# A later q, sums on GpSimd and a grouped weight decode in the prologue of an attention and expert kernel

## The chip, the cores and the metric

One core of a Trainium2 chip runs the whole kernel. The metric is the device time of one execution in microseconds. Three runs of the kernel before gave 1012.68, 1017.62 and 1015.35 us, median 1015.35.

## What is computed

For 8 batches of 8 heads, 576 tokens and 64 head dimensions, attention goes through 32 memory slots; its output is the input of two expert layers.

```
a    = softmax(phi, over the 576 tokens)
k_m  = a^T k;  v_m = a^T v                      # 32 slots per head
attn = softmax(q k_m^T / 8, over the 32 slots)
x    = attn v_m                                 # 4608 tokens x 512
y    = max(x w1, x w2, x w3) w_out              # 512 -> 768 -> 512
out  = the expert of the largest gate: relu(y e_w1) e_w2, times its gate
```

The weights w1, w2, w3, w_out and the experts' are float64 in memory.

## The kernel before, in words

Every product with float32 data is made of three float32r products of a high and a low part: `mm3` (L99) issues them, `split` (L95) makes the parts, the high one as a copy on ScalarE, the low one as a subtraction on VectorE (on GpSimd for h of batches 1 to 7).

The kernel has two stages: attention with the first expert layer, batch by batch (L889), then the second layer (L981). A batch's attention output stays in its factored form: `at_out` gives the attention weights in `at_hi`, `at_lo`; `u_step` (L407) multiplies one sixth (index f) of w1, w2, w3 with v_m into `u`; `m1_step` (L435) multiplies both for one f, one half of the tokens (hf) and one of the three matrices (i). Matrix 0's result is copied to `hx` by ScalarE (L448), those of 1 and 2 go into `hx` as a running maximum on VectorE (L450); then hx is split. `m2_step` or, for half of batch 0, `m2_by_f` multiplies with w_out. The results of all these products share four PSUM banks.

Weights come as 24 parts of 512 KB: parts 3f, 3f+1, 3f+2 are w1, w2, w3 of index f, parts 18 to 23 are w_out. Each is loaded by the SP queue into one of six raw buffers (L180, `bufs=NRAW`), and decoded from 64-bit words in five instructions: an absolute value on ScalarE (L150), then on VectorE two steps with one input (L153, L160) and two with two inputs (L163, L166). w_out's parts are also split. `w_done(n)` writes the decode of part n and, from part 2 on, the load of part n+6. Parts 0 to 5 are decoded ahead of the batches, while the attention of batch 0 runs; parts 6 to 23 in batch 0's m1 steps, three per f (L916), 6 and 7 only after batch 0's scores (`scored`). `after(t, src)` is a one-element copy on ScalarE into a tile: what overwrites the tile must wait for it, and it waits for src.

The attention of batch b+1 is written between the products of batch b. A `Stream` (L758) holds pairs of a due time and a function; each product step advances its time (0.97 per m1 step), and what is due is written there. The due times are in AT (L56) and, for batch 1, AT1 (L58). In batch 0's stream the loads of phi, k, v and q of batch 1 are added with their own due times and conditions (L895 to L897): phi after part 10 is decoded, k and v after part 13, q after part 15. `load_next_q(b)` (L393) loads q of batch b+1 at the due time of batch b's last q transpose (L370): batch 2's q is loaded with batch 1's attention, that is, during batch 0's products. `prefetch` (L399) does so for phi, k and v.

`at_asum` (L252) sums the exponentials over nine chunks by `over_chunks` (L214): four two-input instructions over 512, 256, 128 and 128 columns, on VectorE; the same helper gives the maxima. `at_qT` (L310) transposes one of four q tiles on VectorE.

The order in which each engine gets its instructions is not the written one: a planner goes by its own estimate of when inputs and engine are ready, and by the written order among those that are. The order is fixed when the program is built; on the chip every engine works down its list.

Of the kernel before, what the change touches and what calls it, by code (L numbers as in the profile page):

```python
# [8 lines left out]
F32 = mybir.dt.float32  # L9
# [10 lines left out]
def kernel(  # L20
# [37 lines left out]
    AT1 = dict(max=18, col=19, sub=20.5, q=(30, 31, 32, 33), exp=22, asum=23, km=31, kvT=33, sc=36,  # L58
               smax=(38, 39.5), sexp=(39.5, 41), ssum=(42, 44), out=(45, 47))
    XN = 256  # L60
# [111 lines left out]
    wraw, wdst = {}, {}  # L172

    def w_load(n, src=None):
        if n >= len(wparts):
            return
        part = wparts[n]
        if isinstance(part, tuple):
            f, i = part
            t = sp.tile([P, J, P], U64, tag="w64", name="w64", bufs=NRAW)  # L180
            if src is not None:
                after(t.bitcast(F32)[:, 0, 0:1], src)
            nc.sync.dma_start(
                out=t, in_=(w1, w2, w3)[i][:, f * P:(f + 1) * P].rearrange("(j p) f -> p j f", p=P)
            )
            t = t.rearrange("p j f -> p (j f)")
        else:
            t = sp.tile([P, DM], U64, tag="w64", name="w64", bufs=NRAW)
            nc.sync.dma_start(out=t, in_=w_out[part * P:(part + 1) * P, :])
        wraw[n] = t  # L190

    def w_dst(n):
        part = wparts[n]
        if n in wdst:
            return
        if isinstance(part, tuple):
            wdst[n] = w123[:, part[0], part[1]].rearrange("p j f -> p (j f)")
        else:
            wdst[n] = sp.tile([P, DM], F32, tag="wod", name="wod", bufs=2)

    def w_a(n):
        w_dst(n)
        decode_a(wdst[n], wraw[n])

    def w_b(n):
        part = wparts[n]
        decode_b(wdst[n], wraw[n])
        if not isinstance(part, tuple):
            split(wo_hi[:, part], wo_lo[:, part], wdst[n])
# [4 lines left out]
    def over_chunks(dst, t, op):  # L214

        h = ep.tile([P, J, 4, M], F32, tag="hc", name="hc")
        nc.vector.tensor_tensor(out=h, in0=t[:, :, 0:4], in1=t[:, :, 4:8], op=op)
        nc.vector.tensor_tensor(out=h[:, :, 0:2], in0=h[:, :, 0:2], in1=h[:, :, 2:4], op=op)
        nc.vector.tensor_tensor(out=dst, in0=h[:, :, 0], in1=t[:, :, 8], op=op)
        nc.vector.tensor_tensor(out=dst, in0=dst, in1=h[:, :, 1], op=op)  # L220

    def at_max(b):
        t = inp["phi", b]
        mx = ep.tile([P, J, M], F32, tag="mx", name="mx")
        over_chunks(mx, t, ALU.max)
        st["mx", b] = mx
# [25 lines left out]
    def at_asum(b):  # L252
        t = inp["phi", b]
        asum = ep.tile([P, J, M], F32, tag="mx", name="asum")
        over_chunks(asum, t, ALU.add)
        st["asum", b] = asum
# [53 lines left out]
    def at_qT(b, j):  # L310

        if ("qT", b) not in st:
            st["qT", b] = ep.tile([P, J, NCH, 2, 32], F32, tag="qT", name="qT")
        nc.vector.transpose(
            out=st["qT", b][:, j].rearrange("p c e d -> p (c e d)"), in_=inp["q", b, j].rearrange("p c d -> p (c d)")
        )
# [49 lines left out]
    def attention(b):  # L366

        T = AT if b > 1 else AT1
# [7 lines left out]
            (T["q"][J - 1], lambda: load_next_q(b)),  # L376
# [16 lines left out]
    def load_next_q(b):  # L393
        if b + 1 < B:
            for j in range(J):
                load_q(b + 1, j)
# [421 lines left out]
    with ExitStack():  # L818
        def w_done(n, src=None):
            if src is not None:  # L820
                w_dst(n)
                after(wdst[n][:, 0:1], src)
            w_a(n)
            w_b(n)
            if n >= 2 and n + NRAW < len(wparts):
                w_load(n + NRAW)
# [57 lines left out]
        def start_step():  # L884
            if started[0] < len(wparts):
                w_done(started[0], scored if started[0] < 8 else None)
                started[0] += 1

        for b in range(B):  # L889
            stream = Stream(attention(b + 1) if b + 1 < B else [])  # L890
            if b > 0:
                stream.add([(2, lambda: gate_a(b - 1)), (5, lambda: gate_b(b - 1)), (11.5, lambda: gate_c(b - 1))])
            else:
                done = lambda n: wdst[n][0:1, 0:1]
                stream.add([(10, lambda: load_phi(1, done(10)))])  # L895
                stream.add([(16 + i, lambda i=i: load_kv(1, i, done(13))) for i in range(2)])
                stream.add([(20 + j, lambda j=j: load_q(1, j, done(15))) for j in range(J)])  # L897
            for f in range(NF1):
# [13 lines left out]
                for hf in range(2):  # L912
                    for i in range(3):
                        m1_step(b, f, hf, i)
                        if b == 0 and (hf, i) in ((0, 0), (0, 2), (1, 1)):
                            start_step()  # L916
                        if b == 0 and 0 < f < NF1 - 1 and (hf, i) == (1, 0):
                            u_step(0, f + 1)
                        stream.advance(0.97)
            if b == 0:  # L920
                while started[0] < len(wparts):
                    start_step()
# [135 lines left out]
```

## Time and profile before

| | |
|---|---|
| time of three runs, median | 1015.35 us |
| time of the profiled execution | 1014.16 us |
| its span, first to last instruction | 1012.4 us |
| TensorE busy | 978.7 us (97%) |
| VectorE busy | 562.1 us (56%) |
| ScalarE busy | 370.5 us (37%) |
| GpSimd busy | 149.9 us (15%) |

The span is the time from the first to the last instruction of one execution. Busy shares are over the whole span; matmuls are pipelined and their ends are modelled, so the gaps between them are partly hidden in their busy time. In the rows below PE is TensorE, DVE VectorE, ACT ScalarE, POOL GpSimd, SPq the SP queue; L163 is line 163 of the kernel before, and a value in brackets is the time for which the engine had been idle before an instruction, with what ended it.

### The profile page before, as it was taken

To read this page: it belongs to the slowest core of one execution; us is meant where nothing else is said; L and a number is where in the kernel's file an instruction comes from. 1 tells how busy PE (TensorE), PEld (TensorE's weight loads), DVE (VectorE), ACT (ScalarE), POOL (GpSimd) and SP (SyncE) were. 2 spreads that over 40 slices of the span, in tenths; PEclk is the share of its full clock that TensorE was granted. 3 is DMA by queue.
4 is the path that set the end of the run, shared out by engine and by line. 5 is a ranking of instruction groups with operands and counts; after the bars stand their busy time and mean duration, and the time that the engine had idled before them with its cause. 6 is when DMAs were issued, how large, how long until landed. Compare 5 with 4: busy or idle time off the path is not lost. (4 is left out here: it accounts for less than half of the span.)

```text
span 1012.4 us, 20551 instructions
## 1 busy us (share of the span) xinstructions
PE 978.7 (97%) x8306; PEld 854.6 (84%) x8306; DVE 562.1 (56%) x1289; ACT 370.5 (37%) x808; POOL 149.9 (15%) x259
## 2 busy tenths in 40 slices
PE   7888999999999999999999999999999999999996
PEld 4466788879888898988989989898989898989885
DVE  6889877473674737657165727171717171716341
ACT  2555343333433324334245415050506060604130
POOL 0000012110211102112021130202021212121110
PEclk9899999999999999999999999999999999999999
DMA  8487423132221322110117417171717161615030
GB/s 288 135 259 262 141 66 103 47 130 83 75 92 48 131 83 75 46 47 2 48 61 251 164 40 221 35 226 32 229 32 228 33 212 49 211 45 151 22 110 22
DMA packets 59107, 114.79 MB, mean 113 GB/s; under 512 B 7687, under 2 KB 20999, under 8 KB 59008
## 3 DMA queue, kind: packets, MB, share of 16 engines
q1 hardware_dynamic: 48480, 94.01, 28.5%
q0 software_dynamic: 4768, 9.94, 4.2%
q10 hardware_dynamic: 5760, 9.48, 2.5%
q8 instruction: 67, 1.10, 0.5%
q14 instruction: 32, 0.26, 0.1%
HBM read 94.00 MB, written 19.44 MB: 112 GB/s over the span
## 5 line engine op out<-in xcount | busy, mean ns | idle before, releaser
L100 PE MATMUL ps_m<-at_hi,u_hi 128*128 128x288 f32 x576 | 177.9, 310 | 6.9 <-ACT hx L448 3.2
L102 PE MATMUL ps_m<-at_hi,u_lo 128*128 128x288 f32 x576 | 170.5, 297 | 0.2 <-ACT u_lo L427 0.2
L101 PE MATMUL ps_m<-at_lo,u_hi 128*128 128x288 f32 x576 | 170.3, 296 | 0.1
L100 PE MATMUL ps_x<-yh,w1h 128*128 128x288 f32 (+1 forms) x544 | 160.3, 295 | 0.2 <-DVE xh L617 0.2
L101 PE MATMUL ps_x<-yl,w1h 128*128 128x288 f32 (+1 forms) x544 | 159.9, 294 | 0.0
L102 PE MATMUL ps_x<-yh,w1l 128*128 128x288 f32 (+1 forms) x544 | 159.8, 294 | 0.0
L97 POOL TENSOR_TENSOR h_lo<-hx,h_hi 128x288 fp32r<-128x288 f32 x84 | 72.9, 868 | 466.3 <-ACT h_hi L96 462.3
L100 PEld LDWEIGHTS ps_m<-at_hi,u_hi 128*128 128x128 f32 x576 | 108.2, 189 | 37.3 <-issue 14.2
L646 POOL DMA_DIRECT2D out_dram<-o x144 | 71.1, 500 | 346.2 <-DVE o L643 306.0
L450 DVE TENSOR_TENSOR hx<-hx,ps_m 128x288 f32<-128x288 f32 x192 | 85.5, 448 | 65.2 <-PE ps_m L102 40.9
L100 PE MATMUL ps_m<-h_hi,wo_hi 128*128 128x288 f32 x384 | 115.1, 300 | 1.9 <-DVE hx L450 1.8
L101 PE MATMUL ps_m<-h_lo,wo_hi 128*128 128x288 f32 x384 | 113.2, 295 | 0.0
L102 PE MATMUL ps_m<-h_hi,wo_lo 128*128 128x288 f32 x384 | 113.0, 295 | 0.0
L102 PEld LDWEIGHTS ps_m<-at_hi,u_lo 128*128 128x128 f32 x576 | 108.7, 189 | 1.4 <-ACT u_lo L427 0.7
L101 PEld LDWEIGHTS ps_m<-at_lo,u_hi 128*128 128x128 f32 x576 | 108.7, 189 | 1.2 <-issue 1.0
L643 DVE TENSOR_SCALAR o<-ps_x,scal 128x512 f32<-128x512 f32 x32 | 24.0, 751 | 151.6 <-PE ps_x L102 151.6
L100 PE MATMUL ps_x<-w2h,xh 128*128 128x512 f32 x272 | 107.7, 396 | 0.0
L101 PE MATMUL ps_x<-w2l,xh 128*128 128x512 f32 x272 | 107.5, 395 | 0.0
L102 PE MATMUL ps_x<-w2h,xh 128*128 128x512 f32 x272 | 107.4, 395 | 0.0
L100 PEld LDWEIGHTS ps_x<-yh,w1h 128*128 128x128 f32 x544 | 102.3, 188 | 1.5 <-DVE xh L617 0.5
L101 PEld LDWEIGHTS ps_x<-yl,w1h 128*128 128x128 f32 x544 | 102.1, 188 | 0.6 <-ACT yl L732 0.2
L102 PEld LDWEIGHTS ps_x<-yh,w1l 128*128 128x128 f32 x544 | 102.1, 188 | 0.0
(200 smaller groups left out, 1593.6 us busy)
## 6 DMA issues: line engine op xcount, KB each, us to landing
raw<-in_moe_w_dram SPq DMA_DIRECT2D x72, 512.0 KB, 4.7
raw<-y_dram SPq DMA_DIRECT2D x36, 288.0 KB, 3.1
w<-in_moe_w_dram SPq DMA_DIRECT2D x18, 512.0 KB, 5.1
kv_t<-in_k_dram SPq DMA_DIRECT2D x8, 1152.0 KB, 7.1
kv_t<-in_v_dram SPq DMA_DIRECT2D x8, 1152.0 KB, 9.8
q_t<-in_q_dram SPq DMA_DIRECT2D x32, 288.0 KB, 3.0
y_dram<-y_sb ACTq DMA_DIRECT2D x32, 288.0 KB, 2.1
out_dram<-o POOLq DMA_DIRECT2D x144, 64.0 KB, 1.9
```

Source lines behind the costliest of these rows:

```text
L97: eng.tensor_tensor(out=dst_lo, in0=src, in1=dst_hi, op=ALU.subtract)
L100: nc.tensor.matmul(out=ps, lhsT=hi_l, rhs=hi_r, start=first, stop=False)
L101: nc.tensor.matmul(out=ps, lhsT=hi_l, rhs=lo_r, start=False, stop=False)
L102: nc.tensor.matmul(out=ps, lhsT=lo_l, rhs=hi_r, start=False, stop=last)
L450: nc.vector.tensor_tensor(out=hx[0], in0=hx[0], in1=ps, op=ALU.max)
L643: nc.vector.tensor_scalar(out=o, in0=ps, scalar1=scal[:, b, t:t + 1], scalar2=None, op0=ALU.mult)
L646: nc.gpsimd.dma_start(out=out5[b, half, c], in_=o[i:i + TB])
```

## The change

- Parts 6 to 17, the three matrices of one f, are decoded by one call: four groups, each of one ScalarE and four VectorE instructions over 1536 columns in place of 512. The six raw buffers become one tile with six slots, so that three lie side by side. A group is written at the first m1 step of f = 0 to 3; parts 18 and 19 then follow in f = 3, 20 to 22 in f = 4 and 23 in f = 5. The loads of the three parts that reuse a group's slots are written after the group.
- The sum of exponentials of batch 1 runs on GpSimd.
- q of batch 2 is loaded after batch 1's attention output (at_hi) is there, with a condition on it, in place of with batch 1's q transposes; its four transposes are due at 12.7 to 15.7 in batch 1's stream in place of 0 to 5, and wait for h_hi of batch 1, f = 1. As `load_next_q` goes by the same due times, q of batch 3 is loaded later, too.
- In batch 1's schedule the maximum is due at 17 in place of 18; its phi waits for part 9 in place of 10, k and v for part 12 in place of 13.

```diff
--- before.py
+++ after.py
@@ -55,8 +55,9 @@
 
     AT = dict(max=1, col=4.5, sub=6.5, q=(0, 2, 3.5, 5), exp=9, asum=11, km=16.5, kvT=18, sc=20.5,
               smax=(24.5, 27), sexp=(29, 31), ssum=(34, 37), out=(41.5, 45))
-    AT1 = dict(max=18, col=19, sub=20.5, q=(30, 31, 32, 33), exp=22, asum=23, km=31, kvT=33, sc=36,
+    AT1 = dict(max=17, col=19, sub=20.5, q=(30, 31, 32, 33), exp=22, asum=23, km=31, kvT=33, sc=36,
                smax=(38, 39.5), sexp=(39.5, 41), ssum=(42, 44), out=(45, 47))
+    AT2 = dict(AT, q=(12.7, 13.7, 14.7, 15.7))
     XN = 256
     TT0 = [t * P for t in range(NTT - 1)] + [S - P]
     QK = 1.0 / float(D) ** 0.5
@@ -169,60 +170,59 @@
 
 
     wparts = [(f, i) for f in range(NF1) for i in range(3)] + list(range(NF1))
-    wraw, wdst = {}, {}
+    wdst = {}
+    raw64 = sp.tile([P, NRAW, DM], U64, name="raw64")
 
     def w_load(n, src=None):
         if n >= len(wparts):
             return
         part = wparts[n]
+        t = raw64[:, n % NRAW]
         if isinstance(part, tuple):
             f, i = part
-            t = sp.tile([P, J, P], U64, tag="w64", name="w64", bufs=NRAW)
             if src is not None:
-                after(t.bitcast(F32)[:, 0, 0:1], src)
+                after(t.bitcast(F32)[:, 0:1], src)
             nc.sync.dma_start(
-                out=t, in_=(w1, w2, w3)[i][:, f * P:(f + 1) * P].rearrange("(j p) f -> p j f", p=P)
+                out=t.rearrange("p (j f) -> p j f", j=J),
+                in_=(w1, w2, w3)[i][:, f * P:(f + 1) * P].rearrange("(j p) f -> p j f", p=P),
             )
-            t = t.rearrange("p j f -> p (j f)")
         else:
-            t = sp.tile([P, DM], U64, tag="w64", name="w64", bufs=NRAW)
             nc.sync.dma_start(out=t, in_=w_out[part * P:(part + 1) * P, :])
-        wraw[n] = t
-
-    def w_dst(n):
+
+    def w_dst(n, m):
         part = wparts[n]
         if n in wdst:
             return
         if isinstance(part, tuple):
-            wdst[n] = w123[:, part[0], part[1]].rearrange("p j f -> p (j f)")
+            wdst[n] = w123[:, part[0], part[1]:part[1] + m].rearrange("p i j f -> p (i j f)")
         else:
             wdst[n] = sp.tile([P, DM], F32, tag="wod", name="wod", bufs=2)
 
-    def w_a(n):
-        w_dst(n)
-        decode_a(wdst[n], wraw[n])
-
-    def w_b(n):
+    def w_a(n, m):
+        w_dst(n, m)
+        decode_a(wdst[n], raw64[:, n % NRAW:n % NRAW + m].rearrange("p a f -> p (a f)"))
+
+    def w_b(n, m):
         part = wparts[n]
-        decode_b(wdst[n], wraw[n])
+        decode_b(wdst[n], raw64[:, n % NRAW:n % NRAW + m].rearrange("p a f -> p (a f)"))
         if not isinstance(part, tuple):
             split(wo_hi[:, part], wo_lo[:, part], wdst[n])
 
 
     st = {}
 
-    def over_chunks(dst, t, op):
+    def over_chunks(dst, t, op, eng):
 
         h = ep.tile([P, J, 4, M], F32, tag="hc", name="hc")
-        nc.vector.tensor_tensor(out=h, in0=t[:, :, 0:4], in1=t[:, :, 4:8], op=op)
-        nc.vector.tensor_tensor(out=h[:, :, 0:2], in0=h[:, :, 0:2], in1=h[:, :, 2:4], op=op)
-        nc.vector.tensor_tensor(out=dst, in0=h[:, :, 0], in1=t[:, :, 8], op=op)
-        nc.vector.tensor_tensor(out=dst, in0=dst, in1=h[:, :, 1], op=op)
+        eng.tensor_tensor(out=h, in0=t[:, :, 0:4], in1=t[:, :, 4:8], op=op)
+        eng.tensor_tensor(out=h[:, :, 0:2], in0=h[:, :, 0:2], in1=h[:, :, 2:4], op=op)
+        eng.tensor_tensor(out=dst, in0=h[:, :, 0], in1=t[:, :, 8], op=op)
+        eng.tensor_tensor(out=dst, in0=dst, in1=h[:, :, 1], op=op)
 
     def at_max(b):
         t = inp["phi", b]
         mx = ep.tile([P, J, M], F32, tag="mx", name="mx")
-        over_chunks(mx, t, ALU.max)
+        over_chunks(mx, t, ALU.max, nc.vector)
         st["mx", b] = mx
 
     def at_col(b):
@@ -252,7 +252,7 @@
     def at_asum(b):
         t = inp["phi", b]
         asum = ep.tile([P, J, M], F32, tag="mx", name="asum")
-        over_chunks(asum, t, ALU.add)
+        over_chunks(asum, t, ALU.add, nc.gpsimd if b == 1 else nc.vector)
         st["asum", b] = asum
 
     def at_km(b):
@@ -311,6 +311,9 @@
 
         if ("qT", b) not in st:
             st["qT", b] = ep.tile([P, J, NCH, 2, 32], F32, tag="qT", name="qT")
+        if b == 2:
+
+            after(st["qT", b][:, j, 0, 0, 0:1], hs[1, 1][0].bitcast(F32)[0:1, 0:1])
         nc.vector.transpose(
             out=st["qT", b][:, j].rearrange("p c e d -> p (c e d)"), in_=inp["q", b, j].rearrange("p c d -> p (c d)")
         )
@@ -365,7 +368,7 @@
 
     def attention(b):
 
-        T = AT if b > 1 else AT1
+        T = {1: AT1, 2: AT2}.get(b, AT)
         L = [
             (T["max"], lambda: at_max(b)),
             (T["col"], lambda: at_col(b)),
@@ -373,7 +376,7 @@
         ]
         L += [(T["q"][j], lambda j=j: at_qT(b, j)) for j in range(J)]
         L += [
-            (T["q"][J - 1], lambda: load_next_q(b)),
+            (T["q"][J - 1] if b > 1 else T["out"][1] + 0.2, lambda: load_next_q(b)),
             (T["exp"], lambda: (at_exp(b, 0), at_exp(b, 1))),
             (T["asum"], lambda: at_asum(b)),
             (T["km"], lambda: at_km(b)),
@@ -393,7 +396,7 @@
     def load_next_q(b):
         if b + 1 < B:
             for j in range(J):
-                load_q(b + 1, j)
+                load_q(b + 1, j, st["at_hi", 1].bitcast(F32)[0:1, 1, 0:1] if b == 1 else None)
 
     def prefetch(b):
         if b < B:
@@ -816,14 +819,15 @@
             return t
 
     with ExitStack():
-        def w_done(n, src=None):
+        def w_done(n, src=None, m=1):
             if src is not None:
-                w_dst(n)
+                w_dst(n, m)
                 after(wdst[n][:, 0:1], src)
-            w_a(n)
-            w_b(n)
-            if n >= 2 and n + NRAW < len(wparts):
-                w_load(n + NRAW)
+            w_a(n, m)
+            w_b(n, m)
+            for i in range(n, n + m):
+                if i >= 2 and i + NRAW < len(wparts):
+                    w_load(i + NRAW)
 
         def keep(src, n):
 
@@ -881,10 +885,12 @@
         u_step(0, 1)
         started = [6]
 
-        def start_step():
-            if started[0] < len(wparts):
-                w_done(started[0], scored if started[0] < 8 else None)
-                started[0] += 1
+        def start_step(first):
+
+            m = 3 if started[0] < 3 * NF1 else 1
+            if started[0] < len(wparts) and (first or m == 1):
+                w_done(started[0], scored if started[0] < 8 else None, m)
+                started[0] += m
 
         for b in range(B):
             stream = Stream(attention(b + 1) if b + 1 < B else [])
@@ -892,8 +898,8 @@
                 stream.add([(2, lambda: gate_a(b - 1)), (5, lambda: gate_b(b - 1)), (11.5, lambda: gate_c(b - 1))])
             else:
                 done = lambda n: wdst[n][0:1, 0:1]
-                stream.add([(10, lambda: load_phi(1, done(10)))])
-                stream.add([(16 + i, lambda i=i: load_kv(1, i, done(13))) for i in range(2)])
+                stream.add([(10, lambda: load_phi(1, done(9)))])
+                stream.add([(16 + i, lambda i=i: load_kv(1, i, done(12))) for i in range(2)])
                 stream.add([(20 + j, lambda j=j: load_q(1, j, done(15))) for j in range(J)])
             for f in range(NF1):
                 if f + 1 < NF1 and b > 0 and f > 0:
@@ -913,13 +919,13 @@
                     for i in range(3):
                         m1_step(b, f, hf, i)
                         if b == 0 and (hf, i) in ((0, 0), (0, 2), (1, 1)):
-                            start_step()
+                            start_step((hf, i) == (0, 0))
                         if b == 0 and 0 < f < NF1 - 1 and (hf, i) == (1, 0):
                             u_step(0, f + 1)
                         stream.advance(0.97)
             if b == 0:
                 while started[0] < len(wparts):
-                    start_step()
+                    start_step(True)
                 start.close()
                 mo["sy"] = late.enter_context(tc.tile_pool(name="sy", bufs=1))
             for hf in range(2):
```

## Rows read from the trace of the kernel before

**Rows 1.** Busy time (and instructions) of PE, PEld, DVE, ACT, POOL; clock, DMA share, GB/s.

```profile
44.00:99.00 55.00, 45.94 (x450) 37.44 (x451) 50.97 (x116) 29.88 (x71) 0.00 (x0) 0.97 0.69 228
...
99.00:125.00 26.00, 25.77 (x239) 20.58 (x240) 22.76 (x45) 11.35 (x28) 0.00 (x0) 1.00 0.50 156
...
125.00:175.00 50.00, 49.19 (x598) 42.66 (x597) 38.15 (x96) 20.70 (x54) 10.38 (x12) 1.00 0.28 93
```

**Rows 2.** Waits, TensorE, 44 to 110 us: total, times, longest.

```profile
PE ps_m L100 <- DVE hx L450: 4.0, 6, 0.9
```

**Rows 3.** Groups of VectorE, 44 to 106 us: count, busy us, mean ns, idle before.

```profile
L163 DVE SCALAR_TENSOR_TENSOR w<-w,w 128x512 uint32<-128x512 uint32 x12 | 8.2, 684 | 0.0
...
L160 DVE TENSOR_SCALAR w<-w 128x512 uint32<-128x512 uint32 x11 | 4.6, 421 | 0.0
...
L97 DVE TENSOR_TENSOR h_lo<-hx,h_hi 128x288 fp32r<-128x288 f32 x12 | 5.5, 455 | 2.5 <-ACT h_hi L96 2.5
```

**Rows 4.** Timeline of VectorE, 58 us and 105 us: start, duration in us, what.

```profile
58.31 0.69 DVE L163 SCALAR_TENSOR_TENSOR w<-w,w 128x512 uint32<-128x512 uint32 x1
...
58.91 0.43 DVE L160 TENSOR_SCALAR w<-w 128x512 uint32<-128x512 uint32 x1
...
59.25 0.69 DVE L166 SCALAR_TENSOR_TENSOR w<-w,w 128x512 uint32<-128x512 uint32 x1
...
104.65 0.46 DVE L450 TENSOR_TENSOR hx<-hx,ps_m 128x288 f32<-128x288 f32 x1
```

**Rows 5.** Timeline of VectorE, at 40 us.

```profile
40.06 0.75 DVE L352 TENSOR_REDUCE ssm<-sc 128x18 f32<-128x576 f32 x1 [0.81 <-ACT sc L347]
```

**Rows 6.** Timeline of ScalarE, 37 to 40 us.

```profile
37.42 0.67 ACT L150 ACTIVATE w<-w 128x512 f32<-128x512 f32 x1
...
39.34 0.69 ACT L347 ACTIVATE sc<-sc 128x576 f32<-128x576 f32 x1
```

**Rows 7.** Timeline of VectorE, first and last of the four additions.

```profile
81.99 0.69 DVE L217 TENSOR_TENSOR hc<-phi_t 128x512 f32<-128x512 f32 x1
...
85.38 0.29 DVE L220 TENSOR_TENSOR asum<-asum,hc 128x128 f32<-128x128 f32 x1
```

**Rows 8.** Timeline of GpSimd, at 132 us.

```profile
131.84 0.80 POOL L97 TENSOR_TENSOR h_lo<-hx,h_hi 128x288 fp32r<-128x288 f32 x1 [3.00 <-ACT h_hi L96]
```

**Rows 9.** Timeline of VectorE, 131 to 134 us.

```profile
131.86 0.83 DVE L518 TENSOR_TENSOR gsh<-glg,gmx 128x40 f32<-128x40 f32 x1
...
133.19 0.20 DVE L525 TENSOR_TENSOR goh<-w,gi 128x40 f32<-128x40 f32 x1
```

**Rows 10.** Timeline of VectorE, 108 to 121 us.

```profile
108.76 0.74 DVE L314 STREAM_TRANSPOSE qT<-q_t 128x576 f32<-128x576 f32 x1
...
120.84 0.76 DVE L97 TENSOR_TENSOR at_lo<-aT,at_hi 128x576 fp32r<-128x576 f32 x1 [0.31 <-ACT at_hi L96]
```

**Rows 11.** Timeline of TensorE, first product of batch 1.

```profile
124.45 0.29 PE L100 MATMUL ps_m<-at_hi,u_hi 128*128 128x288 f32 x1
```

**Rows 12.** Timeline of the SP queue, q loads.

```profile
97.78 18.29 SPq L144 DMA_DIRECT2D q_t<-in_q_dram  x7
```

**Rows 13.** Timeline of ScalarE, two weight steps that waited for loads.

```profile
52.33 0.68 ACT L150 ACTIVATE w<-w 128x512 f32<-128x512 f32 x1 [1.42 <-DMA w<-in_moe_w_dram]
...
70.74 0.66 ACT L150 ACTIVATE wod<-w 128x512 f32<-128x512 f32 x1 [2.72 <-DMA w<-in_moe_w_out_dram]
```

**Rows 14.** Timeline of VectorE, at 72 us.

```profile
71.77 0.46 DVE L97 TENSOR_TENSOR h_lo<-hx,h_hi 128x288 fp32r<-128x288 f32 x1 [1.83 <-ACT h_hi L96]
```

**Rows 15.** Timeline of TensorE, 72 to 79 us.

```profile
72.78 0.40 PE L100 MATMUL ps_m<-at_hi,u_hi 128*128 128x288 f32 x1 [1.82 <-ACT hx L448]
...
76.23 0.44 PE L100 MATMUL ps_m<-at_hi,u_hi 128*128 128x288 f32 x1
...
76.47 0.44 PE L101 MATMUL ps_m<-at_lo,u_hi 128*128 128x288 f32 x1
```

**Rows 16.** Busy time of PE, PEld, DVE, ACT, POOL; clock, DMA share, GB/s.

```profile
70.00:80.00 10.00, 7.04 (x44) 5.53 (x44) 7.28 (x17) 5.62 (x16) 0.00 (x0) 0.83 0.94 358
```

## The prediction

> **What bounds the kernel now.** I read the busy time by stretches first. TensorE is busy 25.77 of 26 us from 99 us on, then 49.19 of 50; before that, in the 55 us in which batch 0's first expert products run, it is busy 45.94 us and VectorE 50.97 [rows 1]. So this stage belongs to VectorE, all later ones to TensorE, and mainly what shortens the stage from 44 us on can shorten the kernel. TensorE's waits agree: its commonest one there is for the running maximum hx on VectorE, 4.0 us in six waits [rows 2]. What fills VectorE is the weight decode: the grouped lines show its steps at 0.42 us with one input and 0.68 with two, eleven and twelve of each kind for the three first matrices alone [rows 3], and each matrix takes two steps of either kind. Batch 0's last maximum starts at 104.65 [rows 4], where the stage ends. The reader is to see that VectorE works down a fixed list; each microsecond taken off it before about 105 us moves the TensorE-bound rest forward, as long as nothing else takes the lead.
>
> **Three matrices at once.** Eight VectorE instructions per group of three go away, the elements stay. What an instruction costs beyond its elements is read off starts: a two-input step is followed 0.60 us after its start, 0.09 before its end, a one-input step 0.34 after its start [rows 4]. A two-input instruction of 288 columns takes 0.455 us, one of 512 takes 0.684 [rows 3]: 1.02 ns a column, so (an estimate) 0.684 + 1024 x 1.02 ns = 1.73 us for 1536, the next start at 1.64, in place of 3 x 0.60 = 1.80. That is 0.08 per instruction saved; for one-input steps, 0.07 (0.34 less 512 columns at half of 1.02 ns). Eight times some 0.07 is 0.55 us per group; four groups (parts 6 to 17) give 2.2 us. Bounds: 0, if dependent steps now stand back to back and wait for one another, and 3.0, if the whole overlap of 0.09 falls away each time. I take 2.2, as the rows have it. Against it: part 8 could be decoded as it came, ahead of batch 0's scores; in one instruction with 6 and 7 it waits for them. Two one-input steps, 0.7 us at most, move into the full stage, half of that out of otherwise idle time: 0.3.
>
> **The idle piece before the stage.** At 40.06 VectorE had waited 0.81 us for the second exponential [rows 5], which ScalarE ran at 39.34, after a decode step of 0.67 us taken up at 37.42 [rows 6]. A group cannot stand there yet, since the third of its matrices has not landed. I take 0.8 us of gain; bounds 0 (other ScalarE work stays in front of the exponential) and 1.5 (it starts right at 37.4, and what waits behind it follows).
>
> **Sums of exponentials on GpSimd.** VectorE loses four additions, the first of 0.69 us, the last of 0.29 [rows 7], some 1.7 together, 1.3 without the overlaps. On GpSimd 288 columns take 0.80 us [rows 8], so 512, 256, 128 and 128 take at most 1.42 + 0.71 + 0.36 + 0.36 = 2.9 us in proportion. GpSimd has nothing else between 44 and 125 us [rows 1], and only four small matmuls behind the sums of k and v read the result: its slowness is covered. Not covered is what it does to VectorE. A subtraction of 40 columns that VectorE began at 131.86, just after GpSimd's addition at 131.84, took 0.83 us and ended with it; its like at 133.19 took 0.20 [rows 8, 9]. So a two-input VectorE instruction stands while GpSimd adds, and about half of the instructions in the full stage are such. VectorE may stand up to 2.9 us: net from -1.6 to +1.3. I take half, 1.4, and so about nothing for this part. The Trainium skill, "GPSIMD Engine Reference", section Key points, says that GpSimd shares its SBUF interfaces with VectorE and contends with instructions of two SBUF inputs and with those in a 2-port mode. By that one-input decode steps could stand as well, and this part would be the full loss of 1.6; no row here has such a step beside GpSimd.
>
> **Batch 2's q.** Four transposes of 0.7 us leave the stretch from 108.76 on, ahead of batch 1's lo parts, the last of which VectorE starts at 120.84 [rows 10]; TensorE starts with them at 124.45, when batch 0's products are through [rows 11]. There are 2.9 us of slack, so leaving is worth 0 now; it keeps the slack if TensorE comes earlier, and were that cover gone, the four would cost 2.8. They arrive behind batch 1's second hi part, some 14 us into that batch, where VectorE is idle 11.85 of 50 us [rows 1]: 0, or up to 2.8 if each displaces a maximum that TensorE waits for. I take 0.3. Four loads leave the SP queue, in which they and batch 3's four stood 18.29 us from 97.78 on [rows 12]. They come to stand behind batch 2's phi, after 121 us, some 15 us before they are read; batch 3's four follow batch 2's transposes, beside batch 3's phi, k and v, and are needed a batch later. Eight one-element copies join ScalarE, which is idle 29.3 of those 50 us [rows 1]. All of these: 0. Batch 1's maximum one step earlier, its phi behind part 9's group and k and v behind part 12's: loads shift by a few us either way. 0 here; the rivals hold the rest.
>
> **Sum.** 2.2 - 0.3 + 0.8 + 0 - 0.3 = 2.4 us of gain. The profiled execution took 1014.16 us (span 1012.4 and 1.8 around it), 1.2 below the median, 1015.35. 1014.2 - 2.4 = 1011.8 us. The bounds together reach from a loss of 5.1 to a gain of 5.8.
>
> **Rival 1: a larger gain.** At 70.74 ScalarE had stood 2.72 us for a weight load [rows 13]; VectorE stood 1.83 behind it [rows 14], TensorE 1.82, and ten of TensorE's products from 76.23 on then started 0.24 us apart in place of 0.13 [rows 15], some 1.2 us more: the granted clock of that stretch is 0.83, so partly the lower level, 1.2 GHz [rows 16]. Three loads issued together may be there in time, and this goes: 1.8 to 3.0 more, and 1.3 with GpSimd's lock missing. That is 4.2 to 6.7 us, 1007.5 to 1010.0. For it: VectorE, not the load, is what TensorE mostly waits for. Against: the DMA engines are 0.94 busy there [rows 16], and k and v now come at the same time as w_out's first parts.
>
> **Rival 2: slower.** ScalarE runs in order. A group's first step waits for the last of three loads, and behind it stand the first copies of hx, without which VectorE's list and TensorE's four banks stop. 1.42 us of such waiting at 52.33 left no idle row on TensorE, 2.72 left 1.82 [rows 13, 15]; between the two lies the point from which it decides. An event costs 1.8 + 1.2 + 0.8 (one more wait for hx, the mean of the six is 0.7) = 3.8 us. Three in place of one (parts 12, 15 and w_out's first): 7.6 - 2.4 = 5.2 slower, 1019.4; four: 1023.
>
> **Rival 3: GpSimd's lock eats it.** The additions cost the full 1.6 and the idle piece is not won: 2.2 - 0.3 - 1.6 - 0.3 = 0, 1014.2 us. The page named above speaks for it.
>
> **Chances.** Forecast, a gain of 1 to 4 us: 0.45. Rival 1: 0.28; one event stands for it, and that it goes is not shown. Rival 2: 0.15. Rival 3: 0.12. About 0.5% (5 us) is what a measurement of this kernel can tell from no change. Against the median, faster by that is below 1010.3: nearly all of rival 1 and a little of the forecast, 0.29. Slower is above 1020.4: the heavier half of rival 2 and a loss nobody has named, 0.11. Same: 0.60. The 8-in-10 range goes from 1006.0 (rival 1, with a margin of 1.5 for the bounds of the decode) to 1018.5 (forecast, rival 3, the lightest part of rival 2).
>
> **What would show it.** Right: four groups of 1536 columns, two-input steps near 1.73 us, the idle piece at 40 us gone, batch 0's last maximum some 2 us before 105, batch 1's first product near 122. GpSimd's lock: two-input steps beside its four additions longer by 0.3 us and more. Rival 2: first steps of 1536 columns with over 2 us of idle time released by a DMA, and TensorE's idle time for ScalarE's hx grown by several us. The forecast is wrong if batch 1's first product starts after 124.45, or if time gained there is lost again before 175 us.

## The result, and the profile after

The changed kernel takes 1020.35 us (median of 20 runs, 1014.90 to 1022.75), the kernel before beside it 1014.98 (20 runs, 1007.89 to 1019.20). The ratio is 1.0054, with a 95% interval of 1.0040 to 1.0068: slower, by some 5.4 us. The forecast was 2.4 us faster, and its range ended at 1018.5.

Busy time by the stretches of [rows 1], changed kernel (columns as there):

```profile
44.00:99.00 55.00, 44.53 (x445) 35.91 (x446) 53.17 (x88) 30.49 (x68) 3.53 (x4) 0.98 0.65 233
99.00:125.00 26.00, 25.46 (x242) 21.19 (x242) 18.16 (x38) 9.90 (x30) 0.00 (x0) 0.98 0.27 92
125.00:175.00 50.00, 47.12 (x562) 41.37 (x561) 38.73 (x94) 19.84 (x54) 10.36 (x12) 0.97 0.37 117
```

Two things are to be seen. In the stage from 44 to 99 us VectorE has 28 instructions fewer, but TensorE gets no more done: 44.53 us, from 45.94. And batch 1, which was full (49.19 of 50 us), has a hole of 2 us and a clock below 1.00.

**The prologue.** TensorE's waits from 44 to 110 us, changed kernel (answers to [rows 2]):

```profile
PE ps_m L101 <- DVE hx L453: 4.6, 3, 2.5
PE ps_m L103 <- ACT u_lo L430: 1.5, 1, 1.5
PE ps_u L429 <- ACT u_hi L428: 1.3, 1, 1.3
PE ps_m L101 <- ACT at_hi L97: 1.0, 1, 1.0
```

The rows of the kernel before for the same tiles, beside its 4.0 us for hx on VectorE [rows 2]:

```profile
PE ps_m L100 <- ACT hx L448: 3.2, 3, 1.8
PE ps_m L100 <- ACT at_hi L96: 0.7, 2, 0.4
PE ps_u L426 <- ACT u_hi L425: 0.3, 1, 0.3
PE ps_m L102 <- ACT u_lo L427: 0.2, 1, 0.2
```

Fewer waits for VectorE's hx, three for six, but longer ones; and TensorE now waits longer for u_lo, u_hi and at_hi, all made on ScalarE. One of these, timeline of ScalarE, changed kernel:

```profile
56.48 1.63 ACT L151 ACTIVATE w<-raw 128x1536 f32<-128x1536 f32 x1 [0.89 <-DMA raw<-in_moe_w_dram]
...
58.34 0.86 ACT L430 ACTIVATE u_lo<-ps_u 128x384 fp32r<-128x384 f32 x2
```

ScalarE's step for a group stands in front of u_lo. Timeline of VectorE at the start of the stage, changed kernel:

```profile
42.17 0.96 DVE L154 TENSOR_SCALAR w<-w 128x1536 f32<-128x1536 f32 x1 [0.56 <-ACT w L151]
...
43.71 0.96 DVE L161 TENSOR_SCALAR w<-w 128x1536 uint32<-128x1536 uint32 x1
...
45.28 1.72 DVE L164 SCALAR_TENSOR_TENSOR w<-raw,w 128x1536 uint32<-128x1536 uint32 x1
...
47.58 1.75 DVE L167 SCALAR_TENSOR_TENSOR w<-raw,w 128x1536 uint32<-128x1536 uint32 x1
49.25 0.45 DVE L453 TENSOR_TENSOR hx<-hx,ps_m 128x288 f32<-128x288 f32 x1
```

The whole first group stands ahead of the first maximum, and VectorE waits for it (0.56 us). The last maximum of batch 0 starts at 101.87 (104.65 in [rows 4]), but 1.1 us of this is an earlier start: counted from VectorE's first decode step behind 27.5 us it is 72.9 us, where the four kernels without grouping that are compared below have 71.6 to 74.6. Batch 0's last store of y is issued only 0.21 us earlier, and batch 1's first product starts at 124.23, where 122 was forecast (124.45 before).

**GpSimd's additions.** Timeline of GpSimd, then of VectorE beside it, changed kernel:

```profile
78.69 1.44 POOL L217 TENSOR_TENSOR hc<-phi_t 128x512 f32<-128x512 f32 x1 [77.36 <-ACT phi_t L250]
80.21 0.80 POOL L218 TENSOR_TENSOR hc<-hc 128x256 f32<-128x256 f32 x1
81.09 0.78 POOL L219 TENSOR_TENSOR asum<-hc,phi_t 128x128 f32<-128x128 f32 x1
81.94 0.52 POOL L220 TENSOR_TENSOR asum<-asum,hc 128x128 f32<-128x128 f32 x1
```

```profile
78.90 1.52 DVE L154 TENSOR_SCALAR wod<-wod 128x512 f32<-128x512 f32 x1
80.34 1.22 DVE L167 SCALAR_TENSOR_TENSOR wod<-raw,wod 128x512 uint32<-128x512 uint32 x1
81.48 0.67 DVE L161 TENSOR_SCALAR wod<-wod 128x512 uint32<-128x512 uint32 x1
```

By [rows 3] such steps take 0.42, 0.68 and 0.42 us: 1.9 us are lost beside additions of 3.5 us in all, which saved VectorE about 1.3.

**Batch 1.** Timeline of the SP queue, then of VectorE and of TensorE, changed kernel:

```profile
140.86 5.13 SPq L145 DMA_DIRECT2D q_t<-in_q_dram  x4
146.24 0.38 SPq L131 DMA_DIRECT2D phi_t<-in_phi_dram  x1
146.67 1.27 SPq L139 DMA_DIRECT2D kv_t<-in_k_dram  x1
```

```profile
152.11 0.69 DVE L217 TENSOR_TENSOR hc<-phi_t 128x512 f32<-128x512 f32 x1 [2.18 <-DMA phi_t<-in_phi_dram]
```

```profile
156.66 0.51 PE L417 MATMUL ps_u<-w,vT 64*32 64x384 f32 x1 [2.38 <-DVE sc L338]
```

The same three of the kernel before, where batch 3's q had been loaded in batch 0 [rows 12]:

```profile
146.06 0.38 SPq L130 DMA_DIRECT2D phi_t<-in_phi_dram  x1
```

```profile
150.23 0.69 DVE L217 TENSOR_TENSOR hc<-phi_t 128x512 f32<-128x512 f32 x1 [0.49 <-DMA phi_t<-in_phi_dram]
```

```profile
154.78 0.51 PE L414 MATMUL ps_u<-w,vT 64*32 64x384 f32 x1 [0.69 <-DVE sc L335]
```

Batch 3's four q loads now stand just ahead of batch 3's phi. It is issued only 0.2 us later than before, but takes 5.8 us to land in place of 4.1. The DMA issues from 136 to 156 us, of the changed kernel and of the one before (KB each, median us to landing):

```profile
q_t<-in_q_dram SPq DMA_DIRECT2D x4, 288.0 KB, 3.6
...
phi_t<-in_phi_dram SPq DMA_DIRECT2D x1, 576.0 KB, 5.8
```

```profile
phi_t<-in_phi_dram SPq DMA_DIRECT2D x1, 576.0 KB, 4.1
```

Batch 3's maximum waits for it at the head of VectorE's list; behind it stand the transposes that empty the banks of batch 2's scores (L338), and the next `u_step` needs two of those banks. The clock after that wait, changed kernel:

```profile
155.00:160.00 5.00, 3.34 (x25) 2.48 (x26) 4.97 (x11) 1.99 (x5) 0.81 (x1) 0.79 0.50 193
160.00:165.00 5.00, 5.00 (x35) 5.00 (x34) 4.45 (x11) 1.41 (x4) 0.80 (x1) 0.87 0.12 28
```

Two of TensorE's products in it (timeline of TensorE, changed kernel):

```profile
158.67 0.44 PE L101 MATMUL ps_m<-at_hi,u_hi 128*128 128x288 f32 x1
158.91 0.44 PE L102 MATMUL ps_m<-at_lo,u_hi 128*128 128x288 f32 x1
```

From 158.19 to 161.31 its products start 0.24 us apart, at the lower level, 1.2 GHz; behind that 0.13 us apart again. The thirteen steps make some 1.4 us.

From batch 0's last store of y to batch 1's last one it takes 65.86 us, from 62.23: 3.6 us lost.

### The profile page after: what moved, and what is told of

It is laid out like the page before. It is cut to its first block, busy times and chain, and to the rows that moved or that the text cites. A ratio compares the mean times of both kernels' runs of the same rounds, so it can differ in the third digit from the quotient of the medians.

```text
span 1019.7 us, 20514 instructions
## 1 busy us (share of the span) xinstructions
PE 979.3 (96%) x8306; PEld 856.0 (84%) x8306; DVE 562.3 (55%) x1253; ACT 369.5 (36%) x807; POOL 153.4 (15%) x263
## 5 line engine op out<-in xcount | busy, mean ns | idle before, releaser
L98 POOL TENSOR_TENSOR h_lo<-hx,h_hi 128x288 fp32r<-128x288 f32 x84 | 72.9, 868 | 386.9 <-ACT h_hi L97 365.2
```

The costliest lines, as they stand in the source:

```text
L98: eng.tensor_tensor(out=dst_lo, in0=src, in1=dst_hi, op=ALU.subtract)
```

## The experiments

Each kernel ran beside the kernel before, which is the 1 of every ratio; 0.001 is 1.0 us. The ratios are from 20 executions of the changed kernel and 10 to 12 of the others (6 of run 4), against 17 to 35 of the kernel before. Three figures are read from each trace, which is of one execution: the **prologue**, from the start of VectorE's first decode step behind 27.5 us (at 28.9 to 31.6 us, as batch 0's loads land) to the issue of batch 0's last store of y, **batch 1**, from there to the issue of batch 1's last store, and **TensorE's waits**, all rows of the view of [rows 2] added up (44 to 110 us).

| kernel | ratio, 95% interval | prologue, us | batch 1, us | TensorE's waits, us |
|---|---|---|---|---|
| before | 1 | 95.01 | 62.23 | 9.0 |
| changed | 1.0054, 1.0040 to 1.0068 | 95.94 | 65.86 | 10.6 |
| 1 batch 3's q behind its v | 1.0030, 1.0011 to 1.0049 | 97.73 | 62.46 | 9.7 |
| 2 batch 2's q as before | 1.0022, 1.0005 to 1.0039 | 96.07 | 62.15 | 9.9 |
| 3 sums on VectorE | 1.0036, 1.0020 to 1.0052 | 95.28 | 65.58 | 11.4 |
| 4 single decode | 1.0061, 1.0041 to 1.0081 | 95.76 | 65.62 | 8.3 |
| 5 grouping alone | 1.0022, 1.0007 to 1.0038 | 96.87 | 62.08 | 10.1 |
| 6 grouping alone, last place | 1.0001, 0.9985 to 1.0018 | 92.08 | 62.13 | 7.8 |
| 7 later q alone | 1.0029, 1.0008 to 1.0051 | 93.24 | 64.24 | 8.4 |
| 8 sums on GpSimd alone | 1.0003, 0.9982 to 1.0023 | 92.19 | 62.13 | 8.4 |
| 9 grouping alone, middle place | 0.9988, 0.9968 to 1.0008 | 95.11 | 62.28 | 7.1 |
| 10 threes, not grouped | 1.0030, 1.0016 to 1.0045 | 99.52 | 62.19 | 10.5 |
| 11 later q alone, behind v | 0.9996, 0.9976 to 1.0017 | 94.12 | 62.86 | 9.0 |
| 12 all three mended | 1.0000, 0.9976 to 1.0023 | 93.57 | 62.40 | 7.2 |

Prologues of one and the same code differ by some 2 us between executions (run 1 and the changed kernel: 97.73 and 95.94), so only groups of kernels are compared by it; batch 1 repeats within 0.8 us in the ten kernels without batch 3's q loads just ahead of its phi, and within 1.6 us in the four with them.

**1. Batch 3's q behind batch 3's v.** The changed kernel with

```diff
-(T["q"][J - 1] if b > 1 else T["out"][1] + 0.2, lambda: load_next_q(b)),
+(T["q"][J - 1] if b > 2 else (T["kvT"] + 0.2 if b == 2 else T["out"][1] + 0.2), lambda: load_next_q(b)),
...
-load_q(b + 1, j, st["at_hi", 1].bitcast(F32)[0:1, 1, 0:1] if b == 1 else None)
+load_q(b + 1, j, st["at_hi", 1].bitcast(F32)[0:1, 1, 0:1] if b == 1 else st["vT", 2][0:1, 0:1] if b == 2 else None)
```

> The changed kernel, with batch 3's four q loads issued behind phi, k and v of batch 3 instead of ahead of them. T1 (the four loads ahead of phi(3) delay its landing, VectorE's maximum of batch 3 waits for it and holds up the transposed scores behind it): phi(3) lands in about 4 us instead of 5.8, VectorE's wait before that maximum falls from 2.2 us to about 0.5, TensorE's idle time before the step on the scores from 2.4 to about 0.7, the clock of 155 to 165 us is full again, and the end of batch 1 comes about 3.4 us earlier than in the changed kernel: some 3.4 us off its time, about 1017 where the changed kernel has 1020.4. T1b (batch 2's four transposes, which now stand in batch 1, hold VectorE up, the loads do not matter): nothing moves, batch 1 still ends 3.4 us late, time as the changed kernel.

Timelines of VectorE and of TensorE, this kernel:

```profile
152.51 0.69 DVE L217 TENSOR_TENSOR hc<-phi_t 128x512 f32<-128x512 f32 x1 [0.34 <-DMA phi_t<-in_phi_dram]
```

```profile
157.05 0.51 PE L417 MATMUL ps_u<-w,vT 64*32 64x384 f32 x1 [0.52 <-DVE sc L338]
```

phi of batch 3 lands in 4.0 us, both waits are back to what they were before (0.34 and 0.52 us), batch 1 is 62.46 us long. The four transposes still stand in batch 1, so T1b falls. 2.4 us of the 5.4 are gone from the ratio, where 3.4 were expected; the intervals allow either.

**2. Batch 2's q as before.** The changed kernel with AT2, the later due time and the conditions of `load_next_q` and `at_qT` taken out again.

> The changed kernel with the part on batch 2's q taken back whole: loads, transposes and due times as in the kernel before; grouped decode and sums on GpSimd stay. T1 and T1b: the loss of 3.4 us inside batch 1 is gone, so some 3.4 us off the changed kernel's time; since the prologue gained only 0.2 us, the time is that of the kernel before, within 1 us. If the loss stays, neither the loads nor the transposes made it, and what is left is the shift of batch 1 by the other parts.

Batch 1 is 62.15 us long, the time 3.2 us below the changed kernel's, yet still 2.2 above the kernel before, in the prologue: a second loss.

**3. Sums on VectorE.** The changed kernel with

```diff
-over_chunks(asum, t, ALU.add, nc.gpsimd if b == 1 else nc.vector)
+over_chunks(asum, t, ALU.add, nc.vector)
```

> The changed kernel with batch 1's sums of exponentials back on VectorE. If GpSimd's additions stop VectorE: its three decode steps of 512 columns near 79 to 82 us, which took 1.52, 1.22 and 0.67 us, are back at 0.42, 0.68 and 0.42 (1.8 us less), the four additions cost about 1.3, so VectorE's list is some 0.5 us shorter. If it does not, the three steps stay slow. Total: 0.0 to -0.5 us against the changed kernel, since TensorE's first m2 product at 96.8 waits for a maximum that stands behind w_out's decode; the loss in batch 1 stays.

1.8 us came back, more than the 0.0 to 0.5 expected, though the two intervals overlap. Batch 1's loss stays.

**4. Single decode.** The changed kernel with

```diff
-m = 3 if started[0] < 3 * NF1 else 1
+m = 1
```

> The changed kernel with its matrices' weights decoded one at a time at three places of a half, as in the kernel before; sums on GpSimd and batch 2's q as changed. Theory P (grouping did shorten VectorE's list, by 2.2 us, but brought w_out's parts forward between two maxima, and TensorE gave the gain back in 2.5 us of waiting and a spell at half clock near 97 to 100 us): batch 0's last maximum is back at about 104.5 from 101.9, the wait before the first m2 product back at about 0.9 us, and batch 1 begins within 0.5 us of the changed kernel's. Rival (the gain was lost elsewhere, so grouping is worth its 2.2): batch 1 begins about 2 us later. Either way the loss inside batch 1 stays: about 1020 or 1022 us.

A miss. The last maximum comes at 106.01 us, later than expected, and the ratio is 3 us above what parts 7 and 8 below add up to. It is no clean undoing: batch 1's loads and its maximum keep the due times that were set for groups. At 80.10 TensorE has waited 1.25 us in front of batch 1's product of k and v with phi, which no other run does; the profile puts the wait down to a load of w_out, but what this product reads is k and v, and v, issued at 71.66, takes 8.3 us to land. The granted clock is lower, too: 0.94 from 44 to 99 us and 0.93 to 125 us, where it is 0.97 and 1.00 before. What makes this run so slow stays open.

**5. Grouping alone.** The changed kernel with the edits of 2 and 3 together.

> The changed kernel with the sums of exponentials back on VectorE and batch 2's q as in the kernel before: grouped decode and its due times alone. P (grouping puts up to eight more part-steps of 512 columns ahead of the maxima in VectorE's list, so TensorE waits longer in the middle of the stage, and what the list gains at its end comes when TensorE is no longer waiting for it): the last maximum comes some 1.5 us sooner after the first decode step than before, batch 0's last y is no earlier than before (0 to +0.5 us), no loss in batch 1, total that of the kernel before, within 0.5 us. Rival G (grouping is worth its 2.4 us once the two other parts are gone): batch 0's last y and the total come 2 us or more earlier than the kernel before.

2.2 us slower than the kernel before, where P had expected no difference and G a gain. The last maximum comes no sooner (75.11 us after the first decode step, 74.57 before). The due times of batch 1's loads and maximum are changed here as well. Timeline of ScalarE, then of TensorE, this kernel:

```profile
58.54 1.60 ACT L151 ACTIVATE w<-raw 128x1536 f32<-128x1536 f32 x1 [1.66 <-DMA raw<-in_moe_w_dram]
60.05 0.43 ACT L97 ACTIVATE h_hi<-hx 128x288 fp32r<-128x288 f32 x1
60.38 0.85 ACT L427 ACTIVATE u_lo<-ps_u 128x384 fp32r<-128x384 f32 x2
```

```profile
60.91 0.40 PE L103 MATMUL ps_m<-at_hi,u_lo 128*128 128x288 f32 x1 [2.22 <-ACT u_lo L427]
```

ScalarE's first step of a group waits for three loads and is 1.60 us long; h_hi and u_lo stand behind it in its list, TensorE behind u_lo.

**6. Groups at the last place.** Run 5 with

```diff
-m = 3 if started[0] < 3 * NF1 else 1
+m = 3 if 9 <= started[0] < 3 * NF1 else 1
...
-start_step((hf, i) == (0, 0))
+start_step((hf, i) == (1, 1))
```

and the loads of phi and q of batch 1 behind parts 8 and 12.

> The same with part 6 to 8 decoded one at a time and the groups of three taken up at the last of the three places of a row of products instead of the first, so that no more decode stands ahead of a maximum than in the kernel before (at the eighteen-th maximum 76 part-steps, as before, where the changed kernel has 84); batch 1's phi and q follow parts 8 and 12. P: TensorE's waits for hx in the middle are no longer than before, and the list's gain arrives: batch 0's last y 1 to 2 us earlier after the first decode step than in the kernel before, total 1 to 2 us below it. Rival L (the length of a grouped step of 1.7 us, behind which a maximum stands, is what costs, wherever the group is): no gain, within 0.5 us of the kernel before.

The loss of run 5 is gone, the gain isn't there (1.0001): by the number, L's forecast, which run 9 tests. VectorE works 67.80 us between its first decode step and the last maximum, 69.70 in the kernel before, with equally many part-steps (a part-step is one decode or split instruction of 512 columns, or a third of a longer one). TensorE has other waits, first of them this one (timeline of TensorE, this kernel):

```profile
82.44 0.56 PE L414 MATMUL ps_u<-w,vT 64*32 64x384 f32 x8 [2.47 <-DVE w L167]
```

Groups taken up late are ready late for the `u_step` that reads them.

**7. Later q alone.** The kernel before with AT2, the later due time and the two conditions, nothing else.

> The kernel before with the part on batch 2's q alone. T1: all of the loss of batch 1 (3.4 us) comes from it: phi of batch 3 lands in 5 to 6 us behind the four loads, VectorE waits some 2 us for it, batch 1 is 3.4 us longer, the prologue as before, total 3 to 3.5 us above the kernel before (ratio 1.0033). If batch 1 is as long as before, the loss needs the other parts too.

Timelines of VectorE and of TensorE, this kernel:

```profile
150.68 0.69 DVE L218 TENSOR_TENSOR hc<-phi_t 128x512 f32<-128x512 f32 x1 [1.77 <-DMA phi_t<-in_phi_dram]
```

```profile
155.24 0.51 PE L418 MATMUL ps_u<-w,vT 64*32 64x384 f32 x1 [1.97 <-DVE sc L339]
```

The part makes the loss alone: 2.9 us in the ratio. In this execution batch 1 is longer by 2.0 us, not the 3.4 expected: the wait is 1.97 and the granted clock stays 1.00 behind it.

**8. Sums on GpSimd alone.** The kernel before with `over_chunks` given an engine, GpSimd for batch 1's sums.

> The kernel before with batch 1's sums of exponentials on GpSimd alone. If the two engines stop each other: VectorE's steps beside the four additions take up to three times as long, 1.5 to 2.5 us lost against 1.3 saved; the time is 0.2 to 1.8 us above the kernel before (the changed kernel with the sums back on VectorE was 1.8 below the changed kernel). If only steps with two inputs stood: a gain of up to 0.5 us.

Timeline of VectorE, this kernel:

```profile
78.69 1.50 DVE L153 TENSOR_SCALAR w<-w 128x512 f32<-128x512 f32 x1
```

One step with one input takes 1.50 us beside GpSimd, where it takes 0.42 without. The total is the same within the interval (1.0003). VectorE's steps stand while GpSimd adds, and what is saved and what is lost about balance.

**9. Groups at the middle place.** As run 6, with `(hf, i) == (0, 2)` and the loads of batch 1 as changed.

> Grouping alone, as in the run with late groups (parts 6 to 8 one at a time, q and sums as in the kernel before), but the groups are taken up at the middle one of the three places: 80 part-steps stand ahead of the eighteen-th maximum, where the kernel before has 76 and grouping as changed has 88. P (what stands ahead of the maxima decides): between late groups (1.0001) and groups first (1.0022), nearer to late: 1.000 to 1.001. L (the length of a grouped step decides, wherever it stands): as groups first, 1.002.

0.9988, faster than either, against "between". L's 1.002 lies outside the interval, so P's main point, that the loss goes with the place, stands; parts 6 to 8, decoded one at a time, belong to the place here. The interval includes 1, so no gain is shown.

**10. Threes, not grouped.** Run 5 with

```diff
-w_done(started[0], scored if started[0] < 8 else None, m)
+for i in range(m):
+    w_done(started[0] + i, scored if started[0] < 8 else None)
```

> Grouping alone with the groups at the first place, but each group's three matrices decoded by single instructions of 512 columns, one matrix after the other: the order of the changed kernel without its long instructions and without what they save. P: the order alone costs, so the loss of groups first (2.2 us) stays and the saved overhead (2.2) is missing too: 2 to 4.5 us above the kernel before, ratio 1.002 to 1.0045. L: without long instructions no loss, ratio 1.000 within 0.001.

1.0030, as P had it, and the longest prologue of all, 99.52 us. TensorE's waits from 44 to 110 us, this kernel:

```profile
PE ps_m L101 <- DVE hx L450: 5.2, 5, 2.8
PE ps_m L101 <- ACT hx L448: 1.4, 2, 1.1
```

No instruction here is longer than before, so the order alone makes a loss of this size; L falls. But the waits are others than in run 5: 5.2 us for VectorE's maxima here and 3.1 there, where 3.9 go to u_lo and at_hi (0.7 here). That the order alone costs is shown, that it is the whole of run 5's loss is not.

**11. Later q alone, behind v.** Run 7 with the edit of run 1.

> The kernel before with the part on batch 2's q alone, and batch 3's four q loads issued behind batch 3's phi, k and v. T1: the loss of batch 1 is gone (its length 62 us again, from 64.2 with the loads ahead), the total that of the kernel before within 1 us, since the transposes' slots before and after were not on TensorE's path. T1b (the four transposes inside batch 1 cost): batch 1 stays 2 us or more too long, ratio 1.003.

0.9996, batch 1 62.86 us, VectorE's wait for phi 0.41 us. T1 holds from this side too.

**12. All three mended.** The changed kernel with the edits of runs 1 and 3 and the places of run 9.

> The changed kernel with its three losses taken out: batch 3's q loads behind batch 3's phi, k and v; parts 6 to 8 one at a time and the groups at the middle place; sums of exponentials on VectorE. Theory (the three losses 2.2, 2.9 and 0.3 us add up, and nothing else in the change costs): 5.4 us or more off the changed kernel, at or a little below the kernel before, ratio 0.997 to 1.000; batch 1 62 us long. Rival (a fourth loss that only all parts together make): ratio 1.002 or more.

1.0000: 5.4 us off the changed kernel, and no gain over the kernel before. In no version does the interval end below 1.

## Why the prediction was wrong

The three parts alone cost 2.2 (run 5), 2.9 (run 7) and 0.3 us (run 8): 5.4 together, the whole loss, and run 12, with all three mended, is back at 1.0000. Each of the three carries 1.6 to 2.2 us of uncertainty, so that they add up so exactly is luck. Run 4 doesn't fit the sum.

**"Batch 3's four follow batch 2's transposes, beside batch 3's phi, k and v ... All of these: 0"** failed, and with it more than half of the result (2.9 us). The step named the neighbours and asked when q is needed, a batch later, but not what stands behind it in the SP queue. Shown by runs 1, 2, 7 and 11: with the four loads ahead of phi batch 1 is 64.2 to 65.9 us long, without them 62.1 to 62.9. The size has two pieces: 1.7 us more of TensorE's wait (2.38 less 0.69), and some 1.4 us at the lower clock behind it. The clock fell so in the changed kernel and in runs 3 and 4; in run 7, behind a wait about as long, it did not. The transposes themselves cost batch 1 little, as forecast with 0.3: it is 62.40 to 62.86 us long with them (runs 1, 11, 12), 62.08 to 62.28 without.

**"... each microsecond taken off it before about 105 us moves the TensorE-bound rest forward, as long as nothing else takes the lead"** failed too. The trace of before had a row against the 105 (timeline of TensorE, kernel before):

```profile
98.87 0.40 PE L100 MATMUL ps_m<-h_hi,wo_hi 128*128 128x288 f32 x1 [0.90 <-DVE hx L450]
```

This is TensorE's last wait of a quarter microsecond or more before batch 1: from there on it works through what has piled up, and VectorE's last 6 us don't bound it. Before that row, too, the length of VectorE's list was not what counted: in run 6 VectorE works 1.9 us less, and the time stays.

What the change did instead was to make TensorE wait longer. Its waits add up to 9.7 to 11.4 us in the five kernels with groups at the first place (changed, 1, 2, 3, 5), 8.3 to 9.0 in the five without grouping (before, 4, 7, 8, 11), and 7.1 to 7.8 in the three with groups later (6, 9, 12). Run 10, with the order of the first place but no long instruction, has 10.5. The prologues go the same way: 96.4 us in the mean with groups first, 93.6 without grouping (run 4 left out, which has 95.8), 93.6 with groups later. So the place makes the loss. The changed due times and the one tile for the raw buffers don't make it by themselves: runs 9 and 12 have both and lose nothing.

Which waits they are is less simple. More decode does stand ahead of the maxima: in VectorE's queue 84 part-steps come before the eighteenth maximum, 88 in run 5, 76 before. The first maximum comes 20.3 to 20.9 us after the first decode step in all five kernels with groups at the first place, and 18.0 to 19.0 in all that decode parts 6 to 8 one at a time at three places. Yet TensorE's waits for VectorE's maxima did not grow with groups first (3.9 us in the mean, 4.1 in before, 7, 8 and 11). Those for u_hi, u_lo, at_hi and at_lo did, from 1.4 to 4.5 us, and ScalarE, with the group's step in front, makes all of these but at_lo. So it was in part ScalarE that took the lead. How much of run 5's loss is its long step was not tried by itself.

The Trainium skill, "Perfetto Trace Analysis", section "Identifying the Most-Contended Engine", says to find the engine with the highest occupancy and to optimize it first. In this stage that is VectorE, 50.97 of 55 us [rows 1]; run 6 took 1.9 us off its work and the time stayed. The measurement decides: occupancy named the engine, not which of its instructions TensorE waited for.

**The saved overhead of 2.2 us** was sized rightly: a two-input step over 1536 columns takes 1.72 to 1.75 us (1.73 forecast), and run 6, with three of the four groups, saves VectorE 1.9 us (three times 0.55 forecast). It never reached the end of the stage. With groups first VectorE works as long as before up to its last maximum (69.86 us in the changed kernel, 69.6 to 69.9 in before, 7, 8 and 11), since 102 part-steps stand ahead of it in place of 99. In the three kernels with groups later TensorE's waits are shorter, but the granted clock from 44 to 99 us is 0.90 to 0.94, where before, 7, 8 and 11 have 0.97 to 1.00; what this took back was not separated. **The idle piece before the stage, 0.8**, was not won: VectorE still waits 0.64 us for the second exponential at 38.32, and 0.56 more for the group at 42.17.

**GpSimd's sums, 0 between -1.6 and +1.3**: right in kind and within the bounds in run 8 (0.3 us slower); run 3 and the changed kernel together put it at 1.8, and the runs don't settle between the two. The Trainium skill, "GPSIMD Engine Reference", section Key points, has GpSimd contend with VectorE instructions of two SBUF inputs and with those in a 2-port perf mode; the trace agrees for the step with two inputs, 1.22 us for 0.68. The step with one input stood as well, 1.52 us for 0.42; in which mode it ran, no run shows.

**The rivals.** Rival 2's place was right in part: ScalarE's first step of a group does wait for loads, 0.89 us at 56.48 in the changed kernel and 1.66 in run 5, and TensorE waits behind it, but for u_lo more than for hx, and not at the price that it was given. Rival 3's mechanism is there and gives "same" at most. No rival has the loss as a whole; "a loss nobody has named" was given a share of 0.11 together with the heavier half of rival 2. Of the two signs of being wrong, the second came: batch 1 began 0.2 us sooner, and 3.6 us were lost in it.

## What to carry to other kernels

When a load or a step is moved, read which instructions stand behind it in its new queue, not only when its own result is needed: four small loads that nobody waited for cost 2.9 us through the phi load behind them. In a stage that one engine fills, look at what the other engine waits for, and for the last time, before counting what a shorter list is worth; and see what a longer step pushes back in each queue it stands in, here ScalarE's as well as VectorE's. Grouping instructions changes the order as well as the count; run the order alone, as in run 10, and the same groups at another place, as in run 9, to tell them apart.

## What was not expected of the hardware

A VectorE step with one input of 512 columns took 1.52 and 1.50 us beside a GpSimd addition of 512 columns of 1.44 and 1.32 us, 0.42 without it: it took longer by about the time for which the two overlapped. A running maximum, which has one of its two inputs in PSUM, took 0.44 us beside an addition (at 80.11 in run 8, at 82.07 in the changed kernel), as without one. GpSimd's additions over 512, 256, 128 and 128 columns took 1.44, 0.80, 0.78 and 0.52 us (run 8: 1.32, 0.79, 0.52, 0.53): not in proportion to the columns, which the prediction had assumed.

The later stage, whose code is the same in all kernels, differed between profiled executions: from its first outputs to its last the changed kernel lost 4.4 us against the kernel before, run 3 gained 1.7. A single trace can't place differences of that size there; the ratios of many runs do.
